# Attention with a gated feed-forward: each value product split into two of 64 keys, with a PSUM bank each and six banks left for the rest

## The chip, the cores and the metric

The kernel runs on one core of one Trainium2 chip. The metric is device time in microseconds (us). Two runs of the kernel before took 1749.95 and 1750.27 us, a median of 1750.11 us.

## The reference

The reference normalises x (2048 tokens by 512 features, f32), runs full softmax attention with 32 heads of 16 features on it, runs a gated feed-forward of 1792 hidden features on the same normalised x, and joins the two:

```python
xn = layernorm(x)                                  # 2048 x 512
q, k, v = split(xn @ wqkv)                         # 32 heads of 16
p = softmax(q @ k.T * 16 ** -0.5)                  # per head, 2048 x 2048
s = concat_heads(p @ v) @ wo
g = silu((silu(xn @ w1) * (xn @ w3)) @ w2)         # 1792 hidden features
out = x + s * g
```

## The kernel before

**Phases.** Attention runs in 32 phases: 16 pairs of heads, and for each pair two halves of 1024 queries. A phase needs a row maximum for each of its queries first, and then passes over 16 blocks of 128 keys.

- A *maximum unit* (`max_unit`, L389 and L391) is one TensorE product `m` of 62 rows by 128 queries by 512 keys, and a VectorE `reduce_max` that reads its bank.
- A *score unit* (`scores`, L626 and L629) is one product `e` of 64 rows by 128 keys by 512 queries, and a ScalarE exponential that writes the tile `pt` (128 keys by 512 queries, f32).
- A *value product* (`values`, L639) takes four `pt` tiles: two heads by two blocks of 512 queries. It is four f32 matmuls, each over all 128 keys, with 17 columns of weights (16 values and a one for the softmax sum). Their outputs lie in the same PSUM bank `pv`, on partitions 0, 32, 64 and 96, and are accumulated over the 16 key blocks. The trace shows every one of these matmuls as two, since f32 takes two passes: 8 in a set. There are 512 sets.
- Between these run the products of the feed-forward (`Lanes.emit`, L857), 64 rows by 128 by 512 each, accumulated over many matmuls in one bank `f`.

**Halves of the array.** The products `m`, `e` and `f` use 64 of the array's 128 rows each. The program calls the two halves lane 0 and lane 1; two such products, one on each half, run side by side. They are called half products below. The value products use all 128 rows.

**Order.** The order of TensorE's work is written out by hand: `ORDER_OF_ISSUE` is a string of some 10,000 letters, of which f, s and m are half products of the feed-forward, the scores and the maxima (capitals for lane 1), v is a set of value products, r and R also bring on the small steps of a phase's maxima, and o is work of the last part. A small class (`Model`) keeps estimates of when engines and banks come free; when a letter's work isn't ready by them, it is put off and issued at a later place. A v is issued as soon as its four exponentials are issued; whether `pv` is free is then a wait on the chip.

**Banks.** PSUM has eight banks of 512 f32 here. One is `pv`. Seven (`BANKS`) are shared by `m`, `e`, `f` and the few other products: `take` gives out the one that the estimates say is free first. A load of weights waits until the reader of its bank's former content is done, and TensorE's queue waits behind it.

**End of a phase.** After the last value product of a phase `take_out` copies `pv` with ScalarE to the SBUF tile `ot` (L645; near the end of the program L1213 and L1289 do the same), and the next phase's first set may then write `pv`. The division by the sums and the store follow from `ot`.

**Last part.** The output projection (products `o`, 128 rows by 128 by 512) is interleaved with the last phases.

Of the kernel before, what the change touches and what calls it, by code (L numbers as in the profile page):

```python
# [9 lines left out]
F32 = mybir.dt.float32  # L10
# [7 lines left out]
P = 128  # L18
# [4 lines left out]
NT = S // P  # L23
# [4 lines left out]
VW = DH + 1  # L28
# [8 lines left out]
GH = 4  # L37
RING = 9
AHEAD = 5
HALF = P // 2  # L40
# [100 lines left out]
def raw(ap):  # L141
    return ap.bitcast(F32)
# [3 lines left out]
def kernel(ctx: ExitStack, tc: tile.TileContext, x, wqkv, wo, w1, w3, w2, out):  # L146
    nc = tc.nc
# [4 lines left out]
    psum = ctx.enter_context(tc.tile_pool(name="psum", bufs=1, space=PSUM))  # L152
# [2 lines left out]

    BANKS = 7
    uses = [0] * BANKS
    free_at, was_free, taken_at, kind = [0.0] * BANKS, [0.0] * BANKS, [0] * BANKS, [""] * BANKS  # L160

    def take(v):

        i = min(range(BANKS), key=lambda i: (free_at[i], taken_at[i]))
        uses[i] += 1
# [6 lines left out]
    def bank(v):  # L172
        return take(v)[1]

    pv = psum.tile([P, 512], F32, tag="pv", name="pv", bufs=1)


    xt_d = [[dram.tile([P, KC * 512], F32R, name=f"xt{b}{s}") for s in range(2)] for b in range(TB)]
# [23 lines left out]
    def run(gen):  # L202
        for _ in gen:
            pass
# [91 lines left out]
    mod = Model()  # L296

    class Weights:
# [37 lines left out]
        def next(self):  # L336

            i = self.taken
            self.taken += 1
            self.pump()  # L340
            return i, self.parts.pop(i)
# [11 lines left out]
    vt = {}  # L353
# [5 lines left out]
    def load_v(g):  # L359
        nc.sync.dma_start(room_v(g), v_d[:, :, g * GH * VW:(g + 1) * GH * VW].rearrange("t p (h d) -> p t h d", h=GH))  # L360
# [57 lines left out]
    with tc.tile_pool(name="pro", bufs=1) as pro, tc.tile_pool(name="pros", bufs=1) as pros:  # L418
# [111 lines left out]
        for t in range(4):  # L530
# [6 lines left out]
            xn[t + 2] = norm(t + 2, *of)  # L537
            split_w(KC + t)
            run(products)
        nc.vector.memset(pv, 0.0)  # L540
        for n in range(2):
            nc.vector.tensor_add(picks[:, 2 * n:2 * n + 2], each[:, 0:2], each[:, 2:4])

# [17 lines left out]
        for b in range(TB):  # L561
# [4 lines left out]
            for i, u in enumerate((2, 3, 0, 1) if b == 0 else (2, 0, 1, 3)):  # L566
                t = b * 4 + i
# [30 lines left out]
                r = next(blank, None) if b * TB + i else None  # L598
# [35 lines left out]
    def values(p, half, k, pts):  # L634

        last = (p, half) == LAST
        for j, pt in enumerate(pts):
            key = k * 2 % NT + j // 2 if last else k
            nc.tensor.matmul(pv[32 * j:32 * j + VW, :], vt[2 * p // GH][:, key, 2 * p % GH + j % 2, :], pt,  # L639
                             start=key < 2 if last else k == 0, stop=key >= NT - 2 if last else k == NT - 1)  # L640

    def take_out(p, half):

        ot = work.tile([P, 512], F32, tag="ot", name="ot", bufs=2)
        nc.scalar.copy(ot, pv)  # L645
        yield
        sums = work.tile([P, 16], F32, tag="sums", name="sums", bufs=2)
        rec = work.tile([P, 16], F32, tag="rec", name="rec", bufs=2)
        rd = dram.tile([4, 512], F32, name=f"rd{p * 2 + half}")
        for j in range(4):  # L650
            nc.sync.dma_start(sums[32 * j:32 * j + 32, :], ot[32 * j + DH:32 * j + VW, :])
        yield
        nc.vector.reciprocal(rec, sums)
        yield
        nc.sync.dma_start(rd.rearrange("j (a b) -> (j a) b", b=16), rec)
        yield
        for j in range(4):
            nc.sync.dma_start(rb[32 * j:32 * j + DH, :], rd[j:j + 1, :].to_broadcast([DH, 512]))
        yield
        nc.gpsimd.tensor_mul(ot, ot, rb)  # L660
        oh = work.tile([P, 512], F32R, tag="oh", name="oh", bufs=1)
        ol = work.tile([P, 512], F32R, tag="ol", name="ol", bufs=1)
        nc.gpsimd.tensor_scalar(oh, ot, 1.0, 1.0, op0=ALU.mult, op1=ALU.mult)
        nc.gpsimd.tensor_sub(ol, ot, raw(oh))
        yield
        store_rows(p, half, oh, ol)

    def store_rows(p, half, oh, ol):
        for qb in range(2):
            for h in range(2):  # L670
                j, r = 32 * (qb * 2 + h), (p % 4) * 32 + h * DH
                for s, v in enumerate((oh, ol)):
                    b = half * 2 + qb
                    dst = raw(o_d[p // 4][s][b]) if p < NP - 1 else raw(ov[b][s][p // 4])
                    nc.sync.dma_start(dst[r:r + DH, :], raw(v)[j:j + DH, :])
# [197 lines left out]
    lanes = Lanes()  # L873
    free_at[:] = [0.0] * BANKS
    mod.start()
# [5 lines left out]
    ov, wos, side, sums, there = {}, [], {}, {}, {}  # L881
# [159 lines left out]
    def pt_tile(dtype):  # L1041
        return work.tile([P, 512], dtype, tag="pt", name="pt", bufs=PTS)
# [64 lines left out]
    pv_free = 0.0  # L1107
# [79 lines left out]
    def fresh(at):  # L1187

        return at[2] == 0 or at == (*LAST, NT // 2)
# [4 lines left out]
    def issue_v():  # L1194
        nonlocal pv_free
        c = closed.pop(0)
        p, half, k = c["at"]
        there = max(c["end"], pv_free if fresh(c["at"]) else 0.0)
        values(p, half, k, [c["pts"][j] for j in range(4)])
        if half == 0 and k == 10 and 2 * p % GH == 0 and 0 < 2 * p < H - GH:  # L1200
            load_v(2 * p // GH + 1)
        begins = mod.whole(mod.VALUES, there)
        multiplied[count["V"]] = begins + mod.VALUES + 0.2
        state["seen"] = max(state["seen"], c["last"])
        count["V"] += 1
        j = p * 2 + half
        if k == NT - 1 and j < PHASES - 3:
            g = take_out(p, half)
            next(g)
            outs.append([mod.now + 2.0, g, j, -1])  # L1210
        elif k == (NT - 1 if j < PHASES - 1 else NT // 2 - 1) and j >= PHASES - 3:
            sums[j] = [work.tile([P, 512], F32, tag="ot", name="ot", bufs=2)]
            nc.scalar.copy(sums[j][0], pv)  # L1213
        else:
            return
        pv_free = mod.work("act", begins + mod.VALUES + 0.3, 0.6) + mod.NOTICE
        if j in sums:
            sums[j].append(pv_free)

# [32 lines left out]
    for c in ORDER_OF_ISSUE:  # L1252
        settle()
        small()
        tend()
        catch_up()
        if c in "rR":
            second()
        if c in "rv":
            while not closed:  # L1260
                mod.wait(0.1)
                settle()
                small()
                tend()
                catch_up()
            issue_v()
        elif c == ".":
            mod.wait(mod.SLOT)
        elif c == "o":
            if "o" in late or not projecting():  # L1270
                late.append("o")
        elif c != "R":
            what = (c.lower(), int(c.isupper()))
            if what in late or not half_issued(*what):
                late.append(what)
    while count["V"] < PHASES * NT or len(steps) > 4:
        settle()
        small()
        tend()
        if rows and rows[0][2] == 2 and rows[0][0] <= mod.now:  # L1280
            second()
        if values_ready(mod.now):
            issue_v()
        elif not any(half_issued(what, h) for h in sorted(range(2), key=lambda h: mod.lane[h]) for what in "smf"):
            if not projecting():
                mod.wait(0.1)

    ot, oh, ol = pt_tile(F32), pt_tile(F32R), pt_tile(F32R)
    nc.scalar.copy(ot, pv)  # L1289

    def whole(adder):
        _, b, t = steps.pop(0)
# [48 lines left out]
```

## Time and profile before

| | us |
|---|---|
| two runs | 1749.95 and 1750.27, median 1750.11 |
| span of the profiled execution | 1747.2 |
| what lies around the span, against the median | 2.9 |
| TensorE matmul busy | 1737.2 |
| VectorE busy | 1432.9 |
| ScalarE busy | 1258.9 |
| GpSimd busy | 764.1 |
| sets of value products | from 170.9 to 1725 in the span |

The granted TensorE clock is full in every slice of the span. In the tables PE is a TensorE matmul, PEld a load of its weights, DVE VectorE, ACT ScalarE, POOL GpSimd. A matmul's end is modelled and includes the time in which it runs out of the array, so the matmuls shown overlap: the distance from one start to the next is what counts. L numbers are lines of the kernel before; the changed kernel has the value product on L643, the maxima on L390 and L392, the scores on L628, the feed-forward on L867, the copy of `pv` on L649 and the new addition on L650.

### The profile page before, as it was taken

The page shows a single profiled execution, that of the slowest core. Times are in us where ns is not written, and L with a number is a line of the kernel's source. Part 1 is how long each engine was busy: PE and PEld are TensorE (multiplying, and loading weights), DVE is VectorE, ACT ScalarE, POOL GpSimd, SP SyncE. Part 2 cuts the span into 40 slices and gives each one's busy share as a digit, 9 for nine tenths or more (in the row PEclk, how much of TensorE's full clock was granted, in tenths as well). Part 3 has the DMA queues.
Part 4 walks back from the last instruction along what each step waited for, and adds up shares of the span by engine and source line. Part 5 has one row for each costly group of instructions (what it writes and reads, how often), then busy time and mean ns, then how long its engine had stood idle before and what let it go on. Part 6 is the DMA issues. An engine that isn't in the chain of part 4 may idle for free.

```text
span 1747.2 us, 35524 instructions
## 1 busy us (share of the span) xinstructions
PE 1737.2 (99%) x13188; PEld 1027.4 (59%) x13188; DVE 1432.9 (82%) x2343; ACT 1258.9 (72%) x2440; POOL 764.1 (44%) x791
## 2 busy tenths in 40 slices
PE   9999999999999999999999999999999999999998
PEld 7876655555555555555555565565555565555455
DVE  7576988888888888898888888898888897898625
ACT  4223788778878787778778877788787867868861
POOL 3102744346526561546356452555265615562101
PEclk9999999999999999999999999999999999999999
DMA  8657213132323222231433231132322321331542
GB/s 286 239 200 206 59 41 71 47 71 54 80 76 85 65 56 50 62 81 47 93 98 68 51 80 29 50 68 75 101 80 62 81 39 55 101 93 31 172 155 97
DMA packets 146798, 155.37 MB, mean 89 GB/s; under 512 B 42304, under 2 KB 100672, under 8 KB 143648
## 3 DMA queue, kind: packets, MB, share of 16 engines
q1 hardware_dynamic: 145760, 151.52, 32.0%
q8 instruction: 104, 1.70, 0.4%
q10 hardware_dynamic: 864, 1.57, 0.2%
q14 instruction: 70, 0.57, 0.1%
HBM read 107.97 MB, written 44.02 MB: 87 GB/s over the span
## 4 chain that ended last, share of the span: by engine, by line
PE 92%; issue 4%; DMA 2%; SPq 1%; DVE 0%; ACT 0%; POOL 0%; ACTq 0%; POOLq 0%
PE f L857 27%; PE pv L639 26%; PE e L626 17%; PE m L389 14%; PE m L507 2%; PE e L195 2%; PE e L199 2%; PE e L197 2%; PE m L480 0%; PE m L404 0%; DMA ovl<-o 0%; DMA wl<-g 0%; SPq L894 0%; DMA inh<-in_A_x_dram 0%; DMA last<-in_A_wo_dram 0%
## 5 line engine op out<-in xcount | busy, mean ns | idle before, releaser
L391 DVE TENSOR_REDUCE mp<-m 128x1 f32<-128x512 f32 x2048 | 1301.3, 684 | 192.2 <-PE m L389 123.8
L629 ACT ACTIVATE pt<-e 128x512 f32<-128x512 f32 x2048 | 1091.3, 605 | 301.9 <-PE m L389 130.7
L626 PE MATMUL e<-qs,ks 64*128 64x512 f32 x2048 | 713.2, 413 | 1.8 <-DMA qs<-ml 1.8
L389 PE MATMUL m<-ks,qs 62*128 62x512 f32 x2048 | 691.9, 411 | 0.2 <-DVE mp L391 0.2
L639 PE MATMUL pv<-pt,vt 128*17 128x512 f32 x4096 | 515.0, 597 | 0.0
L626 PEld LDWEIGHTS e<-qs,ks 64*128 64x128 f32 x2048 | 340.1, 184 | 266.8 <-ACT pt L629 87.9
L389 PEld LDWEIGHTS m<-ks,qs 62*128 62x128 f32 x2048 | 337.1, 184 | 123.3 <-ACT pt L629 39.6
L639 PEld LDWEIGHTS pv<-pt,vt 128*17 128x17 f32 x4096 | 81.1, 96 | 202.6 <-issue 194.3
L857 PE MATMUL f<-xtl,wh 64*128 64x512 f32 x488 | 171.8, 391 | 0.0
L857 PE MATMUL f<-xth,wl 64*128 64x512 f32 x488 | 171.7, 396 | 0.0
L857 PE MATMUL f<-xth,wh 64*128 64x512 f32 x488 | 169.0, 392 | 0.0
L742 POOL TENSOR_TENSOR h<-g,h 128x512 f32<-128x512 f32 x56 | 71.9, 1284 | 215.9 <-ACT h L738 215.8
L857 PE MATMUL f<-wh,hs 64*128 64x512 f32 x496 | 148.4, 395 | 0.0
L857 PE MATMUL f<-xth,xel 64*128 64x512 f32 x408 | 147.4, 396 | 0.0
L857 PE MATMUL f<-xth,xeh 64*128 64x512 f32 x408 | 144.7, 393 | 0.0
L857 PE MATMUL f<-xtl,xeh 64*128 64x512 f32 x408 | 143.9, 392 | 0.0
L322 POOL TENSOR_TENSOR wl<-wr,wh 128x512 fp32r<-128x512 f32 x92 | 118.4, 1287 | 7.7
L857 PE MATMUL f<-xeh,hs 64*128 64x512 f32 x400 | 121.5, 393 | 0.0
L321 POOL TENSOR_SCALAR wh<-wr 128x512 fp32r<-128x512 f32 x92 | 56.9, 619 | 115.1 <-PE m L389 47.7
L322 POOL TENSOR_TENSOR xel<-wr,xeh 128x512 fp32r<-128x512 f32 x76 | 97.9, 1288 | 6.3
L726 POOL TENSOR_SCALAR th<-th 128x512 f32<-128x512 f32 x56 | 34.6, 618 | 133.2 <-ACT th L719 133.2
L857 PEld LDWEIGHTS f<-xtl,wh 64*128 64x128 f32 x488 | 85.9, 185 | 6.8
(179 smaller groups left out, 2027.4 us busy)
## 6 DMA issues: line engine op xcount, KB each, us to landing
wr<-in_B_w_dram SPq DMA_DIRECT2D x168, 256.0 KB
qs<-qk SPq DMA_DIRECT2D x186, 64.0 KB
ks<-qk SPq DMA_DIRECT2D x90, 128.0 KB
qk<-sh SPq DMA_DIRECT2D x32, 256.0 KB
qk<-sl SPq DMA_DIRECT2D x32, 256.0 KB
v<-vrow SPq DMA_DIRECT2D x16, 272.0 KB
xin<-in_A_x_dram SPq DMA_DIRECT2D x16, 256.0 KB
g<-part SPq DMA_DIRECT2D x16, 256.0 KB
```

The costliest lines, as they stand in the source:

```text
L195: nc.tensor.matmul(ps, lhs[1], rhs[0], start=first, stop=False)
L197: nc.tensor.matmul(ps, lhs[0], rhs[1], start=False, stop=False)
L199: nc.tensor.matmul(ps, lhs[0], rhs[0], start=False, stop=last)
L321: nc.gpsimd.tensor_scalar(hi, t, 1.0, 1.0, op0=ALU.mult, op1=ALU.mult)
L322: nc.gpsimd.tensor_sub(lo, t, raw(hi))
L389: nc.tensor.matmul(ps, qs[p % 2][64 * h:64 * h + KM, q0:q0 + P], ks[p % 2][64 * h:64 * h + KM, c * 512:(c + 1) * 512], start=True, stop=True)
L391: nc.vector.reduce_max(mp[p, half][:, h, qt, c:c + 1], ps, axis=AX.X)
L626: nc.tensor.matmul(ps, ks[p % 2][64 * h:64 * h + KR, k * P:(k + 1) * P], qs[p % 2][64 * h:64 * h + KR, q0:q0 + 512], start=True, stop=True)
L629: nc.scalar.activation(pt, ps, AF.Exp, scale=DH ** -0.5)
L639: nc.tensor.matmul(pv[32 * j:32 * j + VW, :], vt[2 * p // GH][:, key, 2 * p % GH + j % 2, :], pt, start=key < 2 if last else k == 0, stop= ...
L742: nc.gpsimd.tensor_mul(h2, g, h2)
L857: nc.tensor.matmul(ps, left[r], right[r], start=starts and lane == 0, stop=ends and lane == 1)
```

## The change

Each of the four matmuls of a set becomes two: keys 0 to 63 of the block on the upper half of the array's rows, keys 64 to 127 on the lower half. The two halves add up in two PSUM banks (`pvs[0]` and `pvs[1]`), so the banks for the rest go from seven to six. A set is now 8 matmuls, 16 with the two passes of f32. The four of one half are issued first, then the four of the other. At a phase's end ScalarE copies the first bank to `ot` and VectorE adds the second onto it (`taken`); the estimates count 0.6 us of VectorE there. The order string and the other estimates stay.

```diff
-    BANKS = 7
+    BANKS = 6
...
-    pv = psum.tile([P, 512], F32, tag="pv", name="pv", bufs=1)
+    pvs = [psum.tile([P, 512], F32, tag=f"pv{h}", name="pv", bufs=1) for h in range(2)]
+    pv = pvs[0]
...
-        nc.vector.memset(pv, 0.0)
+        for t in pvs:
+            nc.vector.memset(t, 0.0)
...
     def values(p, half, k, pts):
 
         last = (p, half) == LAST
-        for j, pt in enumerate(pts):
-            key = k * 2 % NT + j // 2 if last else k
-            nc.tensor.matmul(pv[32 * j:32 * j + VW, :], vt[2 * p // GH][:, key, 2 * p % GH + j % 2, :], pt,
-                             start=key < 2 if last else k == 0, stop=key >= NT - 2 if last else k == NT - 1)
+        for lane in range(2):
+            r = slice(HALF * lane, HALF * lane + HALF)
+            for j, pt in enumerate(pts):
+                key = k * 2 % NT + j // 2 if last else k
+                nc.tensor.matmul(pvs[lane][32 * j:32 * j + VW, :], vt[2 * p // GH][r, key, 2 * p % GH + j % 2, :],
+                                 pt[r], start=key < 2 if last else k == 0,
+                                 stop=key >= NT - 2 if last else k == NT - 1)
+
+    def taken(ot):
+
+        nc.scalar.copy(ot, pvs[0])
+        nc.vector.tensor_add(ot, ot, pvs[1])
 
     def take_out(p, half):
 
         ot = work.tile([P, 512], F32, tag="ot", name="ot", bufs=2)
-        nc.scalar.copy(ot, pv)
+        taken(ot)
...
-        pv_free = mod.work("act", begins + mod.VALUES + 0.3, 0.6) + mod.NOTICE
+        pv_free = mod.work("dve", mod.work("act", begins + mod.VALUES + 0.3, 0.6), 0.6) + mod.NOTICE
...
     ot, oh, ol = pt_tile(F32), pt_tile(F32R), pt_tile(F32R)
-    nc.scalar.copy(ot, pv)
+    taken(ot)
```

**One set of value products on TensorE**, in phase 0 of the main part, before (`pv_65` is the bank, `pt_` and a number a tile of exponentials, `vt_` the values; the row ahead is a score product):

```order
L626 MATMUL e_2059<-qs0_132,ks0_134 128x512
L639 MATMUL pv_65<-pt_1934,vt_253 17x512
L639 MATMUL pv_65<-pt_1800,vt_253 17x512
L639 MATMUL pv_65<-pt_1943,vt_253 17x512
L639 MATMUL pv_65<-pt_1887,vt_253 17x512
```

The same set in the changed kernel:

```order
L628 MATMUL e_2069<-qs0_133,ks0_135 128x512
L643 MATMUL pv_65<-pt_1946,vt_254 17x512
L643 MATMUL pv_65<-pt_1802,vt_254 17x512
L643 MATMUL pv_65<-pt_1955,vt_254 17x512
L643 MATMUL pv_65<-pt_1897,vt_254 17x512
L643 MATMUL pv_66<-pt_1946,vt_254 17x512
L643 MATMUL pv_66<-pt_1802,vt_254 17x512
L643 MATMUL pv_66<-pt_1955,vt_254 17x512
L643 MATMUL pv_66<-pt_1897,vt_254 17x512
```

The four tiles of exponentials are read twice, 64 partitions at a time, into two banks.

**Half products around the sets.** On TensorE the sets stand in 387 runs before and 390 after; a run is one set, or several with nothing between them. Of the 386 gaps between the runs before, 238 hold 12 half products or fewer (mostly 6 or 8) and 148 hold 14 or more (mostly 38 to 42). Of the some 8,000 half products only about 14 change places. One of these places, before, is the passage from phase 14 to phase 15, counted from 0 (a row with x4 is a set, the last of phase 14; the row with x8 is two sets, the first of phase 15):

```order
L639 MATMUL pv<-pt,vt 17x512 x4
L389 MATMUL m<-ks_134,qs_132 128x512
L626 MATMUL e<-qs_133,ks_135 128x512
L389 MATMUL m<-ks_134,qs_132 128x512
L626 MATMUL e<-qs_133,ks_135 128x512
L857 MATMUL f<-xtl,xeh 128x512
L626 MATMUL e<-qs_133,ks_135 128x512
L857 MATMUL f<-xth,xeh 128x512
L626 MATMUL e<-qs_133,ks_135 128x512
L639 MATMUL pv<-pt,vt 17x512 x8
```

and in the changed kernel (here a row with x8 is one set):

```order
L643 MATMUL pv<-pt,vt 17x512 x8
L390 MATMUL m<-ks_135,qs_133 128x512
L628 MATMUL e<-qs_134,ks_136 128x512
L390 MATMUL m<-ks_135,qs_133 128x512
L628 MATMUL e<-qs_134,ks_136 128x512
L867 MATMUL f<-xtl,xeh 128x512
L628 MATMUL e<-qs_134,ks_136 128x512
L867 MATMUL f<-xth,xeh 128x512
L643 MATMUL pv<-pt,vt 17x512 x8
L628 MATMUL e<-qs_134,ks_136 128x512
L643 MATMUL pv<-pt,vt 17x512 x8
```

One score product was put off behind the first of the two sets, and a run of two became two runs of one.

**VectorE at the end of the first phase**, before (`mx`, `ml` and `rec` are small steps, `mp<-m` the reductions of the maxima):

```order
L391 TENSOR_REDUCE mp<-m 128x1 x7
L408 TENSOR_TENSOR ml<-m,mh 16x128
L391 TENSOR_REDUCE mp<-m 128x1 x43
L653 RECIPROCAL rec<-sums 128x16
L391 TENSOR_REDUCE mp<-m 128x1 x13
```

and in the changed kernel:

```order
L392 TENSOR_REDUCE mp<-m 128x1 x7
L409 TENSOR_TENSOR ml<-m,mh 16x128
L392 TENSOR_REDUCE mp<-m 128x1 x18
L650 TENSOR_TENSOR ot<-ot,pv 128x512
L392 TENSOR_REDUCE mp<-m 128x1 x23
L663 RECIPROCAL rec<-sums 128x16
L392 TENSOR_REDUCE mp<-m 128x1 x15
```

The addition stands between two reductions; it is there once in each phase. Of the 30 places where one phase of the loop follows another, 10 have 10 half products or fewer between the last set of the one and the first set of the other, and 20 have 38 or more; that is so before and after.

More of the change, by code (lines that the diff above doesn't have):

```diff
@@ L1212, in issue_v @@
             sums[j] = [work.tile([P, 512], F32, tag="ot", name="ot", bufs=2)]
-            nc.scalar.copy(sums[j][0], pv)
+            taken(sums[j][0])
         else:
             return
-        pv_free = mod.work("act", begins + mod.VALUES + 0.3, 0.6) + mod.NOTICE
+        pv_free = mod.work("dve", mod.work("act", begins + mod.VALUES + 0.3, 0.6), 0.6) + mod.NOTICE
         if j in sums:
```

## The prediction

> **What bounds the kernel now.** I read the page's busy times and chain first, then one long stage, then single pieces.
>
> ```profile
> PE 1737.2 (99%) x13188; PEld 1027.4 (59%) x13188; DVE 1432.9 (82%) x2343; ACT 1258.9 (72%) x2440; POOL 764.1 (44%) x791
> ...
> PE 92%; issue 4%; DMA 2%; SPq 1%; DVE 0%; ACT 0%; POOL 0%; ACTq 0%; POOLq 0%
> PE f L857 27%; PE pv L639 26%; PE e L626 17%; PE m L389 14%; PE m L507 2%; PE e L195 2%; PE e L199 2%; PE e L197 2%; PE m L480 0%; PE m L404 0%; DMA ovl<-o 0%; DMA wl<-g 0%; SPq L894 0%; DMA inh<-in_A_x_dram 0%; DMA last<-in_A_wo_dram 0%
> ...
> 600.00:900.00 300.00, 300.00 (x2423) 171.70 (x2423) 259.81 (x423) 237.18 (x459) 140.45 (x143) 1.00 0.28 68
> ```
>
> The chain is TensorE nearly throughout; in the stage of 300 us (columns: PE, PEld, DVE, ACT, POOL busy, clock, DMA share, GB/s) TensorE never stops, at full clock, and VectorE is busy for 259.81 us, 87%. So TensorE's order sets the time, and the readers of its banks have little to spare. These are the groups:
>
> ```profile
> L391 DVE TENSOR_REDUCE mp<-m 128x1 f32<-128x512 f32 x2048 | 1301.3, 684 | 192.2 <-PE m L389 123.8
> L629 ACT ACTIVATE pt<-e 128x512 f32<-128x512 f32 x2048 | 1091.3, 605 | 301.9 <-PE m L389 130.7
> L639 PE MATMUL pv<-pt,vt 128*17 128x512 f32 x4096 | 515.0, 597 | 0.0
> L639 PEld LDWEIGHTS pv<-pt,vt 128*17 128x17 f32 x4096 | 81.1, 96 | 202.6 <-issue 194.3
> ```
>
> One reduction costs VectorE 1301.3 / 2048 = 0.635 us, one exponential ScalarE 1091.3 / 2048 = 0.533 us: banks come free once every 1 / (1/0.635 + 1/0.533) = 0.29 us together.
>
> What value products cost beyond their own streaming is seen in the chain (start, length, piece):
>
> ```profile
> 906.99 0.24 PE m L389 x2
> 907.23 0.98 PE pv L639 x8
> 908.21 0.42 PE e L626
> 908.63 0.23 PE f L857
> 908.86 0.23 PE m L389 x2
> 909.09 0.23 PE f L857 x2
> ...
> 909.33 1.84 PE pv L639 x16
> 911.17 0.43 PE e L626
> ```
>
> A half product's place in a lane takes 0.23 us. A run of two sets takes 1.84, of one 0.98: a further set is 0.86, so 0.12 is the way out of a run. The first half product behind a run takes 0.42 to 0.43 in place of 0.23: 0.20 more. Each run costs 0.32 us that no product uses.
>
> **The change, part by part.**
>
> *The gaps at a run.* With the runs counted in the order (387), they are 387 x 0.32 = 124 us, the one large sum that splitting the rows could touch: with 64-row value products a lane might pass from half products to value products by itself. Do the gaps come from the change of shape, or from the shared rows? This is the same place on the engines:
>
> ```profile
> 906.52 0.39 PE L857 MATMUL f<-xtl,wh 64*128 64x512 f32 x1
> 906.60 0.40 PE L857 MATMUL f<-xth,xel 64*128 64x512 f32 x1
> 906.60 0.23 PEld L389 LDWEIGHTS m<-ks,qs 62*128 62x128 f32 x2
> 906.76 0.47 PE L389 MATMUL m<-ks,qs 62*128 62x512 f32 x2
> 907.16 0.13 PEld L639 LDWEIGHTS pv<-pt,vt 128*17 128x17 f32 x8 [0.33 <-issue]
> 907.16 1.05 PE L639 MATMUL pv<-pt,vt 128*17 128x512 f32 x8
> 908.14 0.18 PEld L626 LDWEIGHTS e<-qs,ks 64*128 64x128 f32 x1 [0.85 <-ACT pt L629]
> 908.25 0.19 PEld L857 LDWEIGHTS f<-xtl,xeh 64*128 64x128 f32 x1
> ```
>
> Within half products a load starts while the lane's former product streams (906.60 against 906.76); behind the set, the load waits until 908.14, when the array is empty. A place near the end shows two shapes that both use all rows, and differ in columns alone:
>
> ```profile
> 1682.03 1.04 PE L639 MATMUL pv<-pt,vt 128*17 128x512 f32 x8
> 1683.00 0.19 PEld L195 LDWEIGHTS o<-ks,ovl 128*128 128x128 f32 x1 [0.85 <-issue]
> 1683.11 0.19 PEld L197 LDWEIGHTS o<-wh,ovh 128*128 128x128 f32 x1
> 1683.34 0.19 PEld L199 LDWEIGHTS o<-ks,ovh 128*128 128x128 f32 x1
> ```
>
> The first load of `o` stays behind the value products with the same 0.85 us, while the next ones start early again (0.11 and 0.23 later). So a change in columns at equal rows empties the array, and from half products (64 rows, 128 columns) to the new value products (64 rows, 17 columns) is such a change. I take the gaps to stay: 0 us. Bounds: -124 us if each lane passes over freely, 0 if nothing changes.
>
> The Trainium skill, "TensorEngine Tiling (Array Packing)", section "Key Properties", says that changing the tiling mode, not just the tile, drains TensorE; it lists 64x128 and 64x32 as different modes. By that rule the gaps stay and this term is 0, without it up to -124 us. The trace agrees at the place above (0.85 us of waiting); the very pair of 64x128 and 64x32 is in no run so far.
>
> *Eight tiles for four.* The loads of a set start together: 8 loads of 0.096 us lie within 0.13 (907.16), so the last starts 0.03 after the first, for four tiles with two passes each. Four more tiles: another 0.03 x 390 runs = 12 us, if the array's two halves work side by side as they do for `f` (906.52 and 906.60). Bounds 0 and 0.03 x 512 = 15.
>
> *Six banks.* At 906.64 the second of the two `m` loads above starts (two loads of 0.19 in 0.23 us). These rows are what ScalarE and VectorE then still have before them:
>
> ```profile
> 904.52 3.04 ACT L629 ACTIVATE pt<-e 128x512 f32<-128x512 f32 x6
> 904.43 4.12 DVE L391 TENSOR_REDUCE mp<-m 128x1 f32<-128x512 f32 x6
> ```
>
> Exponentials end each 0.51 us, so two are unfinished (907.05 and 907.56); reductions each 0.69, so besides this product's own (the last, 908.55) two are (907.18 and 907.86). Two feed-forward products are open, one in each lane. That is six banks, and this load takes the seventh. With six in all it waits for 907.05; its matmul follows 0.11 later (as 908.25 follows 908.14), at 907.16 in place of 906.83 (two of 0.40 in 0.47 from 906.76): 0.33 us, and the value products queued behind it, and all else on TensorE, are late by that. What would hide it is an array kept busy by others, but TensorE's queue waits at that load. VectorE and ScalarE do not gain from it: behind the run they find one result less and run dry earlier. So I charge one release of a bank, 0.29 us, for each of the 148 gaps of 14 half products and more, in which the banks have time to fill, and half of it for the 238 short ones: 43 + 34 = 77 us. Bounds: 0, if the two lanes' slack takes it; 387 x 0.33 = 128. Before the main part and in the last one a bank is turned over in 12 matmuls of 0.23 us, 2.7 us, and six do.
>
> *The end of a phase.* One with little between the phases:
>
> ```profile
> 899.38 0.68 DVE L766 TENSOR_TENSOR part<-part,f 128x512 f32<-128x512 f32 x1
> 899.65 0.59 ACT L645 COPY ot<-pv 128x512 f32<-128x512 f32 x1 [0.61 <-PE pv L639]
> 900.05 1.29 DVE L391 TENSOR_REDUCE mp<-m 128x1 f32<-128x512 f32 x2
> 900.64 0.13 PEld L639 LDWEIGHTS pv<-pt,vt 128*17 128x17 f32 x8 [0.35 <-ACT ot L645]
> ```
>
> The addition (priced as L766's, 0.68) waits for ScalarE's copy until 900.24 and ends at 900.92. First, the next set then starts about 900.99 for 900.64: 0.35 us at the 10 close passages, 4 us; at the others the half products between hide it. Second, the reductions queued behind it on VectorE start 0.87 later, and TensorE's loads wait for their banks: between 0 and 32 x 0.87 = 28 us. VectorE's 13% of free time takes most of that up; I take 8. The second memset is done beside the setup's products: 0, or 0.7 without them.
>
> *Sum.* The span 1747.2 and 2.9 around it are the median, 1750.1. Plus 0, 12, 77, 4 and 8, rounded down: **1850 us**, 5.7% more. With the low ends of the last four and the gaps kept it is 1750, with the high ends 1750 + 15 + 128 + 4 + 28 = 1925.
>
> **The rivals.**
>
> *The gaps go (faster).* If only shared array rows and the same lane's work hold a load back, each lane runs on by itself: -124 us, no offsets to wait for, and 1850 - 12 - 124 = 1714 us; with no loss to banks 1637. It decides from 88 of the 124 us on: 1850 - 12 - 88 is today's 1750. For it: the lanes show independent starts (906.52, 906.60, not in step). Against it: the load at 1683.00. The Trainium skill, "TensorE: Matmul & The Clock Gate", section "Step-by-step: what each phase is for", has TensorE pull a load ahead where the row groups don't conflict or where it fills the background buffer; by that rule this case would come. The trace agrees within one shape (1683.11) and disagrees across shapes (1683.00). Chance 17%, half of it with more than 2% gained.
>
> *Six banks are enough.* The waits lie where a lane would have stood idle anyway, so that the banks cost under 11 us: 1750 + 12 + 4 + 8 = 1774, up to 1785. For it: the order hardly moves (about 14 rows), so the estimates find a bank nearly always. Against: the place at 906.64. Chance 15%.
>
> *Issue becomes the bound.* A set is now 16 loads and 16 matmuls. The densest the trace shows for long is 16 in 0.86 us, 54 ns each, in runs of two sets. If that is TensorE's pace of issue, a set takes 32 x 54 ns = 1.73 us, 0.87 more: 1850 + 512 x 0.87 = 2295. It would also come if the two halves' value products ran one after the other. For it: nothing here is denser. Against: the 8 loads within 0.13 us. Chance 6%.
>
> **How the numbers follow.** A measurement of this kernel tells about 2% (35 us) from no change: faster is below 1715, slower above 1785. The forecast has 62%, all slower. The gaps going: 9% faster, 7% the same, 1% slower. Enough banks: 15% the same. Issue: 6% slower. So faster 0.09, same 0.22, slower 0.69. The range runs from 1715, which leaves the 9% out below, to 1925, which leaves 6% and some of the forecast's own (4%) out above. The likeliest case alone has 1785 to 1925.
>
> **What would show it.** Right: the first load behind a run of `pv` still idles about 0.85 us and a single set's piece in the chain is 1.0 us, not 0.98; the chain shows waits of `m` and `e` on exponentials and reductions; VectorE's busy time grows by 33 x 0.68 = 22 us and its idle time by more. Wrong: loads of half products starting while `pv` streams (the gaps gone), `pv` pieces near 1.7 us (issue), or PE pieces of 0.23 without waits and a time under 1785 (banks enough).

## The result: 2007 us, 14.7% slower, past the upper end of the range

The changed kernel takes 2007.27 us (2006.68 to 2007.86), the kernel before 1750.11 us. The ratio is 1.1472, with a 95% interval of 1.1439 to 1.1506. The direction was forecast; the loss is 257 us where 100 were forecast.

The busy times on the page of the changed kernel:

```profile
PE 1957.5 (98%) x17284; PEld 1067.3 (53%) x17284; DVE 1469.0 (73%) x2377; ACT 1301.0 (65%) x2440; POOL 762.9 (38%) x791
```

VectorE is busy for 36 us more: the additions (22 us), and the reductions, which overlap one another less (686 ns each, after 684). TensorE's busy time grew by 220 us though the half products' work is the same: each of them is shown with 0.39 us or more, so starts that lie some 0.3 us apart, in place of 0.23, still leave no idle time in this view. The groups on the page:

```profile
L392 DVE TENSOR_REDUCE mp<-m 128x1 f32<-128x512 f32 x2048 | 1316.7, 686 | 370.5 <-PE m L390 248.4
L631 ACT ACTIVATE pt<-e 128x512 f32<-128x512 f32 x2048 | 1128.1, 599 | 492.1 <-PE e L628 218.0
L643 PE MATMUL pv<-pt,vt 64*17 64x512 f32 x8192 | 527.8, 594 | 0.0
```

Both readers of the banks take as long for one result as before (686 and 599 ns, after 684 and 605), but stand idle far longer: VectorE 370.5 us in place of 192.2, ScalarE 492.1 in place of 301.9. They wait for TensorE. TensorE in turn waits for them, which the waits of its weight loads show (us in total, times, longest). The kernel before:

```profile
PEld e L626 <- ACT pt L629: 87.9, 110, 0.9
PEld e L626 <- DVE mp L391: 83.1, 100, 2.2
PEld m L389 <- ACT pt L629: 39.6, 52, 0.9
PEld m L389 <- DVE mp L391: 30.8, 50, 0.9
```

The changed kernel:

```profile
PEld e L628 <- ACT pt L631: 160.0, 382, 0.9
PEld e L628 <- DVE mp L392: 145.9, 246, 0.9
PEld m L390 <- ACT pt L631: 112.7, 258, 0.9
PEld m L390 <- DVE mp L392: 70.0, 158, 0.9
```

These rows add up to 312 waits and 241 us before, 1044 waits and 489 us after. They mix two things. The first load behind a run of sets idles 0.85 us whatever the readers do, and the view names the reader that happened to end within that time, as in the row of 1892.47 us further below. Counted by what stands ahead of the load, 269 of the 312 waits (229 us) are such first loads, and 261 of the 1044 (222 us); every one of them is 0.85 us long. What is left is true waiting for a reader: 43 waits of 13 us in all before, 783 waits of 267 us after, 2 for each run of sets, and most of these loads start some 0.05 us after that reader ends. The growth, 254 us, is about as large as the loss.

What value products cost is read from the chain in a stretch near the end (the page's own chain reaches back only some 118 us and is of no use for the whole):

```profile
1888.78 1.86 PE pv L643 x32
1890.64 0.43 PE m L390
...
1891.53 1.01 PE pv L643 x16
1892.54 0.43 PE m L390
```

A run of two sets takes 1.86 (1.84 before), of one 1.01 (0.98), and the half product behind it 0.43 (0.42 to 0.43).

To split the loss, I summed from the starts of all TensorE matmuls of a trace, from the first set on, how long each shape's stretches last, each from its first start to the next shape's first start. Before, the value products' 387 stretches take 488.1 us and the half products' 383 take 1017.1. After, 390 take 500.6 and 384 take 1260.7. So 12 us lie in the value products, and 244 in the half products, whose work is the same. The rest of the span grew by 3 us, nearly all of it ahead of the first set (at 170.9 us before, 173.9 after).

### The profile page after: what moved, and what is told of

Its sections match the earlier page's. It is cut to its first block, busy times and chain, and to the rows that moved or that the text cites. A ratio compares the mean times of both kernels' runs of the same rounds, so it can differ in the third digit from the quotient of the medians.

```text
span 2006.1 us, 43732 instructions
## 1 busy us (share of the span) xinstructions
PE 1957.5 (98%) x17284; PEld 1067.3 (53%) x17284; DVE 1469.0 (73%) x2377; ACT 1301.0 (65%) x2440; POOL 762.9 (38%) x791
## 5 line engine op out<-in xcount | busy, mean ns | idle before, releaser
L392 DVE TENSOR_REDUCE mp<-m 128x1 f32<-128x512 f32 x2048 | 1316.7, 686 | 370.5 <-PE m L390 248.4
L631 ACT ACTIVATE pt<-e 128x512 f32<-128x512 f32 x2048 | 1128.1, 599 | 492.1 <-PE e L628 218.0
L628 PE MATMUL e<-qs,ks 64*128 64x512 f32 x2048 | 789.4, 440 | 19.4 <-ACT pt L631 15.2
L390 PE MATMUL m<-ks,qs 62*128 62x512 f32 x2048 | 758.1, 432 | 19.5 <-ACT pt L631 16.9
L643 PE MATMUL pv<-pt,vt 64*17 64x512 f32 x8192 | 527.8, 594 | 0.0
L643 PEld LDWEIGHTS pv<-pt,vt 64*17 64x17 f32 x8192 | 95.7, 92 | 171.7 <-issue 164.2
L867 PE MATMUL f<-xth,wh 64*128 64x512 f32 x488 | 179.1, 406 | 0.0
L867 PE MATMUL f<-wh,hs 64*128 64x512 f32 x496 | 158.0, 406 | 0.5 <-ACT pt L631 0.5
L867 PE MATMUL f<-xtl,xeh 64*128 64x512 f32 x408 | 153.6, 410 | 0.0
L867 PE MATMUL f<-wl,hs 64*128 64x512 f32 x248 | 92.6, 408 | 0.0
```

The source lines that it names most:

```text
L390: nc.tensor.matmul(ps, qs[p % 2][64 * h:64 * h + KM, q0:q0 + P], ks[p % 2][64 * h:64 * h + KM, c * 512:(c + 1) * 512], start=True, stop=True)
L392: nc.vector.reduce_max(mp[p, half][:, h, qt, c:c + 1], ps, axis=AX.X)
L628: nc.tensor.matmul(ps, ks[p % 2][64 * h:64 * h + KR, k * P:(k + 1) * P], qs[p % 2][64 * h:64 * h + KR, q0:q0 + 512], start=True, stop=True)
L631: nc.scalar.activation(pt, ps, AF.Exp, scale=DH ** -0.5)
L643: nc.tensor.matmul(pvs[lane][32 * j:32 * j + VW, :], vt[2 * p // GH][r, key, 2 * p % GH + j % 2, :], pt[r], start=key < 2 if last else k == 0,
L867: nc.tensor.matmul(ps, left[r], right[r], start=starts and lane == 0, stop=ends and lane == 1)
```

## The experiments

The theory after this reading is *banks*: TensorE's queue waits for banks, and the 64-row value products themselves cost little. The rivals are *split* (the shape, the count or the issue of the value products) and *end of phase* (VectorE standing behind ScalarE's copy). Times are medians; each ratio is against runs of the kernel before on the same chip.

| run | time, us | ratio, 95% interval | half products' stretches, us |
|---|---|---|---|
| before | 1750.1 | | 1017.1 |
| changed | 2007.3 | 1.147 (1.144 to 1.151) | 1260.7 |
| six banks, nothing else changed | 1988.0 | 1.136 (1.135 to 1.138) | 1253.0 |
| five banks, nothing else changed | 2286.7 | 1.307 (1.304 to 1.309) | 1535.4 |
| changed, no addition | 2002.8 | 1.145 (1.143 to 1.147) | 1259.0 |
| changed, banks dealt by reader | 2362.4 | 1.348 (1.345 to 1.352) | 1536.5 |
| changed, other estimates | 2010.4 | 1.150 (1.148 to 1.152) | 1260.6 |
| changed, shorter reductions | 1973.7 | 1.128 (1.127 to 1.130) | 1227.8 |
| before, shorter reductions | 1747.5 | 0.999 (0.998 to 1.000) | 1014.7 |
| changed, shorter exponentials | 1929.5 | 1.103 (1.101 to 1.105) | 1184.9 |
| changed, both over 256 columns | 1863.8 | 1.065 (1.064 to 1.067) | 1119.6 |
| changed, both over 64 columns | 1811.4 | 1.035 (1.034 to 1.037) | 1067.0 |

**Six banks, whole value products.** The kernel before with one number changed (by way of the estimates it also moves some dozens of TensorE's products):

```diff
-    BANKS = 7
+    BANKS = 6
```

> The kernel before with six banks instead of seven and nothing else: value products whole, over 128 rows, one bank pv, no addition on VectorE; the eighth bank lies idle. Theory 'banks' (the loss is TensorE waiting for banks): most of the 257 us, 1950 to 2005 us. Rival 'split' (the 16 short-row matmuls of a set, their issue, or the passage between shapes cost it): at most 1830 us, my priced 77 us for the bank. Rival 'end of phase': between the two, the rest then being the addition.

Measured: 1988.0 us, 238 us over the kernel before. *Split* falls: with no split, no second bank and no addition, 238 of the 257 us are there. The waits of its loads are nearly those of the changed kernel (without the first loads behind a run, 738 waits of 253 us):

```profile
PEld e L626 <- DVE mp L391: 154.1, 261, 0.9
PEld e L626 <- ACT pt L629: 146.0, 347, 0.9
PEld m L389 <- ACT pt L629: 100.0, 226, 0.9
PEld m L389 <- DVE mp L391: 74.1, 164, 0.9
```

**Five banks.**

```diff
-    BANKS = 7
+    BANKS = 5
```

> The kernel before with five banks. Theory 'banks': the sixth bank costs at least as much as the seventh, over 2200 us. Theory 'split': under 1930 us (twice 77 us, with some more).

Measured: 2286.7 us, 299 us more than with six. Each bank costs more than the one before it, as *banks* expected.

**No addition.**

```diff
-        nc.scalar.copy(ot, pvs[0])
-        nc.vector.tensor_add(ot, ot, pvs[1])
+        nc.scalar.activation(ot, pvs[0], AF.Copy, bias=1e-6)
```

> The changed kernel without VectorE's addition at the end of a phase: ScalarE's copy adds a constant 1e-6, the second bank is never read, so keys 64 to 127 of each block are missing from the output. Theory 'banks': 1985 to 2007 us, the addition costs 0 to 22 us. Rival 'end of phase' (VectorE stands behind ScalarE's copy, its reductions and the banks they hold come late): at most 1930 us.

Measured: 2002.8 us. The addition costs 4.4 us. *End of phase* falls. With six whole banks at 1988.0, the split and the addition together are worth 19.3 us: between these two kernels the value products' stretches grow by 11.5 us (489.1 to 500.6) and the half products' by 7.7.

**Banks dealt by reader.** Does TensorE wait for the wrong bank, one chosen ahead by estimates while another lies free?

```diff
-        i = min(range(BANKS), key=lambda i: (free_at[i], taken_at[i]))
+        own = {"m": (0, 1), "e": (2, 3), "f": (4, 5), "o": range(BANKS)}[v]
+        i = min(own, key=lambda i: (free_at[i], taken_at[i]))
```

> The changed kernel with the six banks dealt out by their reader: two for the maxima, two for the scores, two for the feed-forward, each taken in turn. Same number of banks, same order string. If the loss is waiting for the wrong bank (one chosen ahead while another was free): 30 us or more faster than the changed kernel, below 1975 us. If it is the number of banks alone: the division makes it worse, 2007 us or more.

Measured: 2362.4 us, much worse. The granted clock was 0.98 here, 1.00 in the other runs; 2% of the time are 47 us, far from the 355 us by which this run is behind the changed kernel. With two banks each, the maxima's loads are shown to wait 367.3 us for VectorE and the scores' 361.2 us for ScalarE (327 and 270 without the first loads behind a run):

```profile
PEld m L391 <- DVE mp L393: 367.3, 579, 4.4
PEld e L629 <- ACT pt L632: 361.2, 755, 1.2
```

So the estimates' common pool was the better choice. I also laid the banks that the built program gives out beside the changed kernel's trace: of some 1680 loads that start within 0.08 us of the release of their own bank, 34, or 2%, could have had another bank 0.05 us earlier. The waits are for banks that are truly all taken.

**Other estimates.** The estimates were made longer, as the readers are on the chip, and two kinds of work are put off while no bank is expected free:

```diff
-        COST = {"act": 0.495, "dve": 0.605}
+        COST = {"act": 0.53, "dve": 0.685}
...
-            return i - len(self.ended) < 2 and self.begun(i)
+            return i - len(self.ended) < 2 and self.begun(i) and min(free_at) <= mod.now + EARLY
...
-        return any(left[h] for _, left in rooms)
+        return any(left[h] for _, left in rooms) and min(free_at) <= mod.now + EARLY
```

> The changed kernel, full work, with another order: the estimates of a reader's time are raised to 0.53 us (ScalarE) and 0.685 us (VectorE), and a maximum or the start of a feed-forward product is put off where no bank is expected free within 0.5 us, as scores already are. Rival 'order' (the order written for seven banks is the trouble): 60 us or more back, under 1945 us. Theory 'bank time': within 40 us of 2007 us.

Measured: 2010.4 us, no gain. It moves only some dozens of TensorE's products, since the letters still set the order, so it is a weak test of that order; a wholly new one for six banks wasn't tried, and whether it could win back a part is left open.

**Shorter reductions, at six banks and at seven.** If banks are held too long by their readers, a reader that ends sooner must help at six banks and not at seven.

```diff
-        nc.vector.reduce_max(mp[p, half][:, h, qt, c:c + 1], ps, axis=AX.X)
+        nc.vector.reduce_max(mp[p, half][:, h, qt, c:c + 1], ps[:, 0:256], axis=AX.X)
...
-        nc.scalar.activation(pt, ps, AF.Exp, scale=DH ** -0.5)
+        nc.scalar.activation(pt, ps, AF.Exp, scale=DH ** -0.5 / 8)
```

> The changed kernel with VectorE's reductions of the maxima over 256 of their 512 columns, so that each gives its bank back some 0.3 us sooner (half of the keys are left out of the maxima; the exponentials' scale is 1/32 instead of 1/4, which keeps them finite; both make the output another one). Theory 'bank time' (banks are held for a fixed sum of time, and the six of them are at most 76% taken): 2048 x 0.3 = 614 us of 8290 less, the main part 7676 / (6 x 0.762) = 1679 us for 1813, so about 1873 us in all. Rival 'order' (TensorE's queue stands at the wrong bank whatever the readers do): 1975 us or more.

> The kernel before, seven banks, with the same shorter reductions and scale. Theory 'bank time': seven banks just suffice for TensorE, whose own work and gaps are the bound, so 1715 to 1750 us, far less gained than at six. If banks bind at seven as they do at six: 7676 / (7 x 0.762) = 1439 us for 1555, about 1634 us.

Measured: 1973.7 us at six, 34 us less; 1747.5 us at seven, 2 us less than the kernel before on that chip (1749.2). At seven banks VectorE does not bind, as forecast. At six, *bank time* with its fixed share of 76% falls: it gave 1873. What is left waits for the other reader: without the first loads behind a run, the loads' waits for VectorE fell from 59 to 2 us, and those for ScalarE rose from 207 to 243.

**Shorter exponentials, and both.** The exponentials write 256 columns and the value products read them twice (a reshaping of their output is left out here):

```diff
-        nc.scalar.activation(pt, ps, AF.Exp, scale=DH ** -0.5)
+        nc.scalar.activation(pt[:, 0:256], ps[:, 0:256], AF.Exp, scale=DH ** -0.5)
...
-                                 pt[r], start=key < 2 if last else k == 0,
+                                 pt[r, 0:256].rearrange("p (a b) -> p a b", a=1).to_broadcast([HALF, 2, 256]), start=key < 2 if last else k == 0,
```

> The changed kernel with ScalarE's exponentials over 256 of their 512 columns, so that each gives its bank back some 0.2 us sooner; the value products read those 256 columns twice and stream as long as before (half of the queries are left out, the output is another one). Theory 'both readers' (TensorE's queue takes scores and maxima in turn, so the slower reader's bank stops it, whichever it is): like the shorter reductions' 33 us, a gain of 60 us at most, 1945 us or more. Theory 'hold time' (each microsecond of holding counts alike): 2048 x 0.2 us of holding is two thirds of what the shorter reductions took off, so about 22 us, near 1985 us. A gain of over 130 us would make ScalarE alone the cause.

> Both shortened, the reductions of the maxima and the exponentials over 256 of 512 columns (scale 1/32 again, the output is another one), six banks and the split value products kept. Theory 'both readers': far more than the sum of the two alone, 130 us or more back, at most 1875 us. Theory 'hold time': the sum of the two, about 55 us back, near 1950 us. If six banks don't suffice whatever the readers do, 1960 us or more.

Measured: 1929.5 us with the exponentials alone, 78 us less, more than either theory gave; 1863.8 us with both, 144 us less, against 111 for the sum of the two alone. *Both readers* was right on the second and missed the first; *hold time* missed both. That the shorter exponentials win more than the shorter reductions fits the 207 us of waiting for ScalarE against 59 for VectorE, though no run shows that as the cause. The two readers do hold each other's work up, though less strictly than one stopping all.

**Both over 64 columns.**

```diff
-        nc.vector.reduce_max(mp[p, half][:, h, qt, c:c + 1], ps[:, 0:256], axis=AX.X)
+        nc.vector.reduce_max(mp[p, half][:, h, qt, c:c + 1], ps[:, 0:64], axis=AX.X)
...
-        nc.scalar.activation(pt[:, 0:256], ps[:, 0:256], AF.Exp, scale=DH ** -0.5 / 8)
+        nc.scalar.activation(pt[:, 0:64], ps[:, 0:64], AF.Exp, scale=DH ** -0.5 / 8)
```

> As the run with both readers over 256 columns, but over 64 (scale 1/32, the value products read the 64 columns eight times; the output is another one), six banks, split value products, the same order. If the reader's time is what holds the banks too long, the half products' waits shrink once more: from 1864 us to 1810 us or less. If what is left there (114 us over the kernel before) is something else, such as the 0.43 us between a product's start and its reader's, which no shorter reading takes away, it stays above 1835 us.

Measured: 1811.4 us, 52 us less again (1 us short of the first case's mark, far from the second's). The groups show both readers at a third of their time:

```profile
L392 DVE TENSOR_REDUCE mp<-m 128x1 f32<-128x64 f32 x2048 | 435.9, 223 | 991.0 <-PE m L390 718.4
L631 ACT ACTIVATE pt<-e 128x64 f32<-128x64 f32 x2048 | 437.8, 226 | 931.8 <-PE e L628 517.9
```

So 196 of the 257 us go with the readers' time alone, six banks and split kept. Of the other 61 us, 19 are the split's and the addition's. Some 42 remain, and their cause is open: with the banks, the 0.5 us that lie on average between a product's start and its reader's start in this run may play a part, but no run shows that by itself.

**One value product, 17 or 128 columns.** Does a gap stand at each change of shape, and at nothing else? Both runs issue only the first of a set's four value products on each half of the rows (`pts[:1]`); the second also widens the weights to the half products' 128 columns. In both the rows of `pvs` that nothing writes start as ones, and the exponentials' scale is 1/32:

```diff
-                nc.tensor.matmul(pvs[lane][32 * j:32 * j + VW, :], vt[2 * p // GH][r, key, 2 * p % GH + j % 2, :],
+                nc.tensor.matmul(pvs[lane], vt[2 * p // GH].rearrange("p t h d -> p (t h d)")[r, 64 * key // 2:64 * key // 2 + P],
```

> The changed kernel with only the first of the four value products of a set, on both halves of the rows, 17 columns of weights (the other three are left out of the output, scale 1/32). If a change of shape empties the array: the first load behind a run idles until the array is empty, about 0.09 us after the last pass has streamed, 0.52 us after that pass's start.

> As the run with one value product of 17 columns, but with 128 columns of weights (other values beside the 17, so that the output is another one): the same shape as the half products, nothing to change over. If the change of shape makes the gap: the load behind the value products starts while they stream, 0.2 us or more before their end, and up to 0.32 us a run, 387 runs, 124 us, comes back against the run with 17 columns, less what waiting for banks eats. If two-pass value products by themselves make the gap (the load of a two-pass product isn't taken ahead): the same idle time and the same total as with 17 columns.

Measured, one run each: 1992.9 us with 17 columns, 1892.1 with 128: 101 of the 124 us that the gaps were counted at. The loads behind a run of two sets, in the run with 17 columns:

```profile
1001.70 0.10 PEld L643 LDWEIGHTS pv<-pt,vt 64*17 64x17 f32 x2 [0.33 <-issue]
1002.65 0.18 PEld L628 LDWEIGHTS e<-qs,ks 64*128 64x128 f32 x1 [0.85 <-DVE mp L392]
```

And behind one set with 128 columns (two halves by two passes, x4):

```profile
1005.79 0.30 PEld L643 LDWEIGHTS pv<-pt,vt 64*128 64x128 f32 x4
1005.79 1.13 PE L643 MATMUL pv<-pt,vt 64*128 64x512 f32 x4
1006.32 0.19 PEld L628 LDWEIGHTS e<-qs,ks 64*128 64x128 f32 x1 [0.23 <-ACT pt L631]
1006.35 0.79 PE L628 MATMUL e<-qs,ks 64*128 64x512 f32 x1
```

With equal shapes the scores' load starts at 1006.32 while the second pass still streams, until about 1006.75: the score product beside it is shown with 0.79 us, 0.40 more than one that streams at once. With unequal shapes the load stays idle for 0.85 us, as 391 first loads behind a run do in the run with 17 columns, and none with 128. The gap belongs to the change of shape.

## Why the prediction was wrong, step by step

**What bounds the kernel: right, but not followed to its end.** TensorE's order set the time, and the readers had "little to spare". That the banks were as tight was in the trace before. Laying the built program's banks beside that trace, 2052 of the 4007 loads of scores and maxima from the first set to the last, 51%, find every bank but their own in use. In the very stretch that the prediction read, six of the eight loads from 904.66 to 906.64 us do, each some 0.05 us after its own bank came free. The prediction looked at the last of them.

**The gaps at a run, 0: right.** The changed kernel shows the pair of shapes that no run had shown:

```profile
1891.46 0.16 PEld L643 LDWEIGHTS pv<-pt,vt 64*17 64x17 f32 x16 [0.36 <-issue]
1891.47 1.07 PE L643 MATMUL pv<-pt,vt 64*17 64x512 f32 x16
1892.47 0.18 PEld L390 LDWEIGHTS m<-ks,qs 62*128 62x128 f32 x1 [0.85 <-ACT pt L631]
```

The first load behind the set idles 0.85 us as before. The rule of the Trainium skill, "TensorEngine Tiling (Array Packing)", "Key Properties", that a change of tiling mode drains the array, agrees with this row's 0.85 us and with the two runs with one value product. The Trainium skill, "TensorE: Matmul & The Clock Gate", section "Step-by-step: what each phase is for", has loads pulled ahead of running matmuls; here that holds within one shape only, as 1006.32 against 1002.65 shows. The rival *the gaps go* is refuted.

**Eight tiles for four, 12: right.** The value products' stretches grew by 12.5 us; the 16 loads of a set lie within 0.16 us (1891.46), and the two halves work side by side. The rival *issue becomes the bound* is refuted by the same 1.01 us a set.

**Six banks, 77 with bounds 0 and 128: the step that failed.** It measured 238 us. The mechanism was the right one, a load of TensorE waiting for a bank with all work queued behind it. The size was wrong because I "charge one release of a bank, 0.29 us, for each of the 148 gaps of 14 half products and more" and half of it for the short ones, as if the missing bank were met once, at the run's start. 77 us are 267 such waits; the loads' true waits for a reader grew by 740, to 0.34 us each on average. The trace shows the missing bank met again and again within a stretch (start, length, loads of the changed kernel):

```profile
1004.09 0.18 PEld L628 LDWEIGHTS e<-qs,ks 64*128 64x128 f32 x1 [0.18 <-ACT pt L631]
1004.09 0.18 PEld L867 LDWEIGHTS f<-xel,hs 64*128 64x128 f32 x1
1004.45 0.18 PEld L390 LDWEIGHTS m<-ks,qs 62*128 62x128 f32 x1 [0.17 <-DVE mp L392]
1004.45 0.18 PEld L867 LDWEIGHTS f<-xel,hs 64*128 64x128 f32 x1
```

Loads follow 0.36 us apart in place of 0.23, and with each of them a feed-forward load on the other half, which needs no new bank, starts only when the waiting one does. Beyond their matmuls' own time (half their number times 0.2285 us, the distance of two products in one lane), the long stretches took 47.5 us before and 192.6 after, 1.03 us more for each of 141; the short ones 55.2 and 153.6, 0.40 us more for each of 243. That is over three times and nearly three times what I charged; with six whole banks the two sums are 184.8 and 153.8, so it is not the split. The upper bound, 0.33 us for each run, was no bound for the same reason. Within a burst one release does not end the waiting, since both readers take longer for a result (0.635 and 0.533 us) than TensorE to make it: two half products in 0.23 us, half of them the feed-forward's, are one score and one maximum in 0.46. Before the first set, where the prediction charged nothing, six whole banks cost 3 us more (the first set at 174.2 us for 170.9).

**The end of a phase, 4 + 8: too high, and small.** It measured 4.4 us in all; VectorE's free time (69 of the 300 us from 600 to 900 us in the changed kernel, 40 before) was enough to take up the delayed reductions, though no run shows that by itself.

**The rival "six banks are enough"** is refuted by the run with six banks alone. The rest of the sum and the direction held; the range's upper end, 1925, fell short by 82 us: its bank term by 110 (238 for 128), while its other terms were 28 too high.

## What to carry to other kernels

Where a producer with one queue in order runs ahead of two slower readers, each buffer carries part of every burst: before one is given up, count in the trace how often the last free one is taken. That count is a warning and not a price: one wait of 0.29 us for each burst, half for the short ones, gave 77 us here, one for each of the 2052 loads would have given 595, and 238 were measured; what settles it is a run with one buffer less and nothing else changed. When reading waits, set those aside that a change of shape makes, since the view may name a reader for them. A bank taken from seven cost 14%, the next one 17%, while the split and the addition for which it was given up cost 1%. And row halves don't free value products of the cost of passing between shapes: that cost is paid by the shape, not by the rows.

## What the runs showed of the hardware

- Eight f32 products on tiles of 64 rows by 17 columns run beside each other as four of 128 rows did: 1.01 us a set with its way out, for 0.98.
- The passage between shapes costs the same whether rows, columns or both change: the first load comes about 0.09 us after the last pass has streamed (0.52 us after that pass's start, 0.43 of it streaming), at 128 by 17 to 64 by 128, at 64 by 17 to 64 by 128 and at 128 by 17 to 128 by 128 alike. It shows as 0.85 us of idle loads at 387 places before.
- A reduction over 64, 256 and 512 columns of a bank takes VectorE 223, 420 and 686 ns, an exponential ScalarE 226, 385 and 599 ns: about 1.03 and 0.83 ns a column, and, by the same line, some 0.16 and 0.17 us that do not depend on the columns.
